# The first layer of three 512-row expert blocks as seven products of halves

## The chip, the cores and the metric

The kernel runs on one core of one Trainium2 chip. The metric is the time of one execution on the device in microseconds (us), from the first to the last instruction with what the launch puts around it. A time "of the runs" is the median of several executions; a profiled execution is a single one, with its own time.

## The reference

A Fourier mixing of eight sequences is followed by a layer of eight experts, of which each row uses one.

```python
# x: (8, 2496, 256)
X = np.fft.fft(np.fft.fft(x, axis=1), axis=2)
x = X.real.reshape(19968, 256)              # rows for the experts
logits = x @ w_gate                         # (19968, 8)
expert_idx = np.argmax(logits, axis=1)
gate_w = softmax(logits)[np.arange(N), expert_idx]
for e in range(8):                          # rows of expert e
    h = np.maximum(x_sorted[lo:hi] @ w1[e], 0.0)   # 256 -> 1024
    y_sorted[lo:hi] = h @ w2[e]                    # 1024 -> 256
out = gate_w[:, None] * y_sorted[inv_perm]
```

All of it is in float32. Only the counts of rows per expert depend on the data.

## The kernel before, in words

**Mixing.** Each of the eight batches of 2496 rows is transformed in two steps. `first(b)` folds the input on VectorE (tile `xq`, lines 307 to 324), multiplies by waves on TensorE (PSUM tile `s1`), copies to `t1` on ScalarE and writes it to DRAM (`Td`). `regroup` reads it back as `t4s`. `second(b)` works on 128 transformed rows at a time: two products `p2` (shown as `p<-table,t4s`), a copy to `zz`, two products `p3` (`p<-table,zz`), copies `zs` and `lg` on ScalarE, the rows themselves on VectorE (line 480) and their mirrored half on ScalarE (line 454). `turn_last` is a small product `pr` and its copy. After five such groups `route` picks each row's expert (`oh`), finds its rank among the rows of that expert by the products `rk`, and queues ten sends. `send` (line 532) copies an index on ScalarE (`due`), casts it on GpSimd (`pi`) and scatters 128 rows to the buffer `Xs` in DRAM, where rows of one expert lie together. `plan` (line 548) then makes, on one partition, the table of blocks of the next round.

**Experts.** The rows of a batch, as far as they fill whole blocks, are worked on in the round of that batch: batch 2 has three blocks of 512 rows of one expert, batches 3 to 7 five each (the first two batches and the tail use blocks of 256 and 128). `experts` is a generator that runs over the blocks. For each block it fetches rows (`xb`, line 606) and weights (`w1_sb`, `w2_sb`, 1 MB each) through the SyncE queue, some blocks ahead; `turn` (line 648) transposes `xb` to `xT` on VectorE (line 654) and negates the odd half on ScalarE (line 657). The first layer then makes `hT` from `xT` and the weights, the second makes `py` from `hT`, which ScalarE scales to `y` (line 962) and GpSimd scatters to the output.

**Two ways for the first layer.** The plain way (lines 899 to 914) makes, for each of eight tiles of 128 hidden units, `ph` with two instructions of 512 columns; ScalarE and VectorE take turns with the relu (lines 910 and 908). The other way is `seven` (line 685): the contraction (256), the hidden units (1024) and the rows (512) are halved, and seven products of halves take the place of eight. For that, `right` makes four sums of parts of `xT` (lines 642 to 645) and `Left` four of parts of the weights (line 637), all on VectorE. Two passes `g` of seven products each accumulate into PSUM tiles `a` to `e`; the results are put together by five additions on VectorE (lines 706, 709, 712, 720, 725) and five copies or relus on ScalarE (703, 716, 717, 722, 726). Which blocks use it says `halved(b, size)`, line 193. `quartered` (line 198) says which blocks do the second layer by seven products too: those that `halved` names in the last batch, or with a number of 3 or more in their batch.

**What sets the order.** Instructions are issued in program order on each engine. The generators of the mixing and of the experts are woven by the loop at line 1066. Each `yield w, full` of `experts` tells how much of a block was done; a yield that isn't `full` adds `ticks * w / ((SHARE if b >= LATE else EARLY) * open_)` to `due`, and each whole tick runs one step of the mixing of the next batches, and for early rounds one send. The steps of `seven` yield `0.5, True`, the plain first layer `1, False`, the second layer `2, False` per 128 rows, or `1, False` twice where `halved`. `open_` (line 1075) counts 8 for a halved block and 16 for another, so that the ticks of a round sum up to the same. When the next block is halved, its `right` comes from `turn`, and its `Left` either from the steps of the present `seven` or, after a plain block, at the end of it (line 967).

**Buffers.** [...] `pm_` has three for all of the mixing, `pse` one for each of the five names `a` to `e`; `ph` uses `a` and `c`, `py` uses `b` and `d`. `xT`, `xs` and `hT` have one buffer each, `ws` two, `xb`, `w1_sb`, `w2_sb` and `y` three, `due` eight.

Of the kernel before, what the change touches and what calls it, by code (L numbers as in the profile page):

```python
# [20 lines left out]
B, S, D = 8, 2496, 256  # L21
# [170 lines left out]

def halved(b, size):

    return size == 512 and b > 2 or size == 256 and b == B - 1


def quartered(b, size, at):

    return halved(b, size) and (b == B - 1 or at >= 3)  # L200
# [17 lines left out]
def kernel(ctx: ExitStack, tc, x, w_gate, w1, w2, out):  # L218
# [429 lines left out]
    def turn(b, size, xb):  # L648


        xT = bp.tile([128, 2, BIG], F32, tag="xT", name="xT", bufs=1)
        n = min(size, 256)
        for h in range(-(-size // 256)):
            vec.transpose(free(xT[:], 256 * h, [32, n // 32], [BIG, 2], [1, 32]),  # L654
                          free(xb, 512 * h, [64, n // 32], [1, 2], [2, 32]))
            odd = xT[:, 1, 256 * h:256 * h + n]
            act.activation(odd, odd, ACTF.Copy, scale=-1.0)  # L657
            yield xT
        if halved(b, size):
            th = size // 2  # L660
            xs = bp.tile([128, 3, th], F32, tag="xs", name="xs", bufs=1)
            r = right(xs, *(xT[:, c, k * th:(k + 1) * th] for c in range(2) for k in range(2)))
            yield r
# [136 lines left out]
    def experts(todo):  # L800
# [44 lines left out]
        for k, (b, size, last, at) in enumerate(todo):  # L845
# [20 lines left out]
            if follow and got and halved(follow[0], follow[1]):  # L866
                more = Left(got[0][0])
# [282 lines left out]
```

## Time and profile before

| | |
|---|---|
| median of three runs | 1253.59 us (1252.57 to 1254.63) |
| the profiled execution, its own time | 1256.62 us |
| its span, first to last instruction | 1254.8 us |
| TensorE clock granted over the span | 0.981 |
| busy TensorE, VectorE, ScalarE, GpSimd | 1210.5, 761.5, 431.8, 448.0 us |
| batch 2's three blocks, first to last product | 238.5 to 338.2 us |
| moved by DMA | 248.32 MB, 198 GB/s |

The profile is of one execution. In the names of engines PE is TensorE, PEld its weight loads, DVE VectorE, ACT ScalarE, POOL GpSimd and SPq the queue of transfers that SyncE issues. A line of a timeline gives the start, the duration, the engine, the line of the kernel, the operation, the tiles (written from read), their shapes and a count; in brackets stands how long the engine was idle before, and what it waited for. All matmuls have line 223, that of a helper, so they are told apart by tiles. A float32 matmul instruction appears as two passes, so that counts of TensorE are twice those of the code. A line of the chain of waits gives the start, the time until the next piece, and the engine and tile that the end of the program hung on. In the rows of digits each digit is the busy share of a fortieth of the span, in tenths.

### The profile page before, as it was taken

The page shows a single profiled execution, that of the slowest core. Times are in us where ns is not written, and L with a number is a line of the kernel's source. Part 1 is how long each engine was busy: PE and PEld are TensorE (multiplying, and loading weights), DVE is VectorE, ACT ScalarE, POOL GpSimd, SP SyncE. Part 2 cuts the span into 40 slices and gives each one's busy share as a digit, 9 for nine tenths or more (in the row PEclk, how much of TensorE's full clock was granted, in tenths as well). Part 3 has the DMA queues.
Part 4 walks back from the last instruction along what each step waited for, and adds up shares of the span by engine and source line. Part 5 has one row for each costly group of instructions (what it writes and reads, how often), then busy time and mean ns, then how long its engine had stood idle before and what let it go on. Part 6 is the DMA issues. An engine that isn't in the chain of part 4 may idle for free.

```text
span 1254.8 us, 22389 instructions
## 1 busy us (share of the span) xinstructions
PE 1210.5 (96%) x7317; PEld 1077.9 (86%) x7317; DVE 761.5 (61%) x1820; ACT 431.8 (34%) x1168; POOL 448.0 (36%) x531
## 2 busy tenths in 40 slices
PE   7569999999999999999999999999999999999997
PEld 5458888777788899889988899889999999999996
DVE  4745334343556787566865488686888884444663
ACT  2334333333244433434343433432332332222222
POOL 0426336163126421471226612471463241111112
PEclk8779999999999999999999999999999999999998
DMA  8679899873649443763347435443446238788887
GB/s 235 186 257 347 293 310 309 229 255 99 150 154 271 135 141 119 203 217 112 101 129 216 134 115 172 134 156 98 126 134 192 93 114 302 271 282 292 277 285 270
DMA packets 163062, 248.32 MB, mean 198 GB/s; under 512 B 118542, under 2 KB 130200, under 8 KB 143473
## 3 DMA queue, kind: packets, MB, share of 16 engines
q1 hardware_dynamic: 145644, 201.79, 50.8%
q0 software_dynamic: 16080, 42.85, 9.6%
q10 hardware_dynamic: 1221, 2.24, 0.6%
q8 instruction: 59, 0.97, 0.3%
q14 instruction: 58, 0.48, 0.1%
HBM read 193.45 MB, written 53.45 MB: 197 GB/s over the span
## 4 chain that ended last, share of the span: by engine, by line
PE 65%; issue 17%; DVE 8%; DMA 4%; POOL 3%; ACT 2%; SPq 0%; POOLq 0%; DVEq 0%; ACTq 0%
PE py L223 19%; PE a L223 9%; PE c L223 8%; PE ph L223 7%; PE p L223 6%; PE b L223 5%; PE d L223 4%; PE e L223 3%; PE s L223 3%; POOL out_dram L238 3%; DMA xq<-in_x_dram 2%; DVE xT L654 1%; DMA Td<-t 1%; DMA t4s<-Td 1%; DVE y L754 1%
## 5 line engine op out<-in xcount | busy, mean ns | idle before, releaser
L238 POOL DMA_INDIRECT out_dram<-y,ro x163 | 161.6, 991 | 627.6 <-ACT y L750 302.9
L223 PE MATMUL py<-w_sb,hT 128*128 128x256 f32 x1504 | 340.0, 380 | 0.4 <-DVE hT L908 0.4
L223 PEld LDWEIGHTS py<-w_sb,hT 128*128 128x128 f32 x1504 | 281.3, 190 | 37.6 <-issue 1.0
L238 POOL DMA_INDIRECT Xs<-rows,pi x160 | 161.8, 1011 | 87.5 <-POOL pi L539 42.6
L223 PE MATMUL ph<-xT,w_sb 128*128 128x128 f32 (+2 forms) x992 | 170.9, 328 | 4.7 <-DVE ro L863 4.7
L223 PEld LDWEIGHTS ph<-xT,w_sb 128*128 128x128 f32 x992 | 136.6, 192 | 28.7 <-issue 16.8
L480 DVE SCALAR_TENSOR_TENSOR rows<-p,zs 128x129 f32<-128x129 f32 x160 | 48.8, 347 | 128.2 <-ACT lg L478 122.1
L223 PE MATMUL a<-xT,w_sb 128*128 128x256 f32 (+1 forms) x512 | 117.9, 357 | 0.2 <-DVE xT L654 0.2
L908 DVE TENSOR_SCALAR hT<-ph 128x512 f32<-128x512 f32 x43 | 29.7, 691 | 134.5 <-PE ph L223 74.8
L223 PEld LDWEIGHTS a<-xT,w_sb 128*128 128x128 f32 x512 | 88.6, 190 | 10.2 <-DVE xT L654 0.6
L962 ACT ACTIVATE y<-py,xb 128x256 f32<-128x256 f32 x94 | 44.6, 474 | 151.5 <-PE py L223 151.3
L657 ACT ACTIVATE xT<-xT 128x256 f32<-128x256 f32 (+1 forms) x94 | 36.5, 389 | 173.8 <-DVE xT L654 131.9
L706 DVE TENSOR_TENSOR hT<-hT,b 128x512 f32<-128x512 f32 x57 | 39.2, 688 | 75.7 <-PE b L223 49.2
L716 ACT ACTIVATE hT<-a 128x512 f32<-128x512 f32 x57 | 34.0, 597 | 134.2 <-PE a L223 129.7
L539 POOL CAST pi<-due 128x1 int32<-128x1 f32 x140 | 43.8, 313 | 70.2 <-ACT due L538 70.2
L223 PE MATMUL a<-w_sb,hT 128*128 128x128 f32 x528 | 66.0, 276 | 0.0
L223 PEld LDWEIGHTS a<-w_sb,hT 128*128 128x128 f32 x528 | 63.1, 192 | 0.7
L223 PEld LDWEIGHTS p<-table,t4s 120*128 120x128 f32 x352 | 54.4, 205 | 10.9 <-ACT t4s L442 3.4
L223 PE MATMUL p<-table,zz 128*128 128x145 f32 (+1 forms) x320 | 57.1, 302 | 5.0 <-DVE rows L480 2.2
L223 PE MATMUL c<-xT,ws 128*128 128x256 f32 (+1 forms) x256 | 60.3, 362 | 0.8
L223 PE MATMUL p<-table,t4s 120*128 120x120 f32 (+1 forms) x352 | 57.8, 290 | 3.4 <-ACT t4s L442 2.6
L223 PE MATMUL b<-xs,ws 128*128 128x256 f32 (+1 forms) x256 | 58.7, 356 | 0.0
(163 smaller groups left out, 2063.6 us busy)
## 6 DMA issues: line engine op xcount, KB each, us to landing
w_sb<-in_moe_w_dram SPq DMA_DIRECT2D x132, 1024.0 KB
xq<-in_x_dram SPq DMA_DIRECT2D x23, 896.0 KB
xb<-Xs SPq DMA_DIRECT2D x112, 128.0 KB
Td<-t SPq DMA_DIRECT2D x18, 448.0 KB
t4s<-Td SPq DMA_DIRECT2D x7, 768.0 KB
t4s<-Td SPq DMA_DIRECT2D x7, 640.0 KB
xb<-Xs SPq DMA_DIRECT2D x52, 64.0 KB
xb<-Xs SPq DMA_DIRECT2D x88, 32.0 KB
```

Of the source, the lines that this page charges most:

```text
L223: nc.tensor.matmul(o, lhsT=lhsT, rhs=rhs, start=start, stop=stop, **kw)
L238: return unordered(pool.indirect_dma_start(out=dst, out_offset=bass.IndirectOffsetOnAxis(ap=idx, axis=0), in_=rows, in_offset=None, bounds ...
L480: vec.scalar_tensor_tensor(rows[:, k + m, 0:NY], p3[:, 0:NY], zs[:, 0:1], zs[:, 1:], op0=ALU.add, op1=op)
L539: pool.tensor_copy(idx, due[:])
L654: vec.transpose(free(xT[:], 256 * h, [32, n // 32], [BIG, 2], [1, 32]), free(xb, 512 * h, [64, n // 32], [1, 2], [2, 32]))
L657: act.activation(odd, odd, ACTF.Copy, scale=-1.0)
L706: vec.tensor_tensor(h12, h11, b[:], op=add)
L716: act.activation(h11, a[:], ACTF.Relu)
L754: vec.tensor_tensor(o, o, p[:], op=add)
L908: vec.tensor_scalar(o, ph[:], 0.0, None, op0=ALU.max)
L962: act.activation(y[:, i % 2], py[:], ACTF.Copy, scale=meta[:, i, 1:2])
```

## The change

`halved` is asked by `turn`, by `experts` and by the loop that weaves. It now says yes for every block of 512 rows, where it did so from batch 3 on. Batch 2 is the only earlier batch with such blocks, so its three blocks use `seven` for the first layer, and the second layer of these blocks yields twice per 128 rows. The numbers of the blocks are 0 to 2, so `quartered` stays false for them.

```diff
 def halved(b, size):
 
-    return size == 512 and b > 2 or size == 256 and b == B - 1
+    return size == 512 or size == 256 and b == B - 1
```

The function that then makes the first layer, as it stands in both kernels (cut):

```python
        for g in range(half // fp):
            a, b, c, d, e = (pse.tile([128, fp, th], F32, tag=k, name=k) for k in "abcde")
            h11, h12, h21, h22 = (q[:, g * fp:(g + 1) * fp] for q in quarters(hT, size))
            product(g, 0, a)
            act.copy(h11, a[:])
            yield
            product(g, 5, b)
            vec.tensor_tensor(h12, h11, b[:], op=add)
            yield
...
            product(g, 2, c, False)
            vec.tensor_tensor(h12, h12, c[:], op=add)
            act.activation(h12, h12, ACTF.Relu)
            ends(g)
            step()
            yield
```

## Prediction

> **What bounds the kernel now.** I read the page's busy times and slices first, then the chain of work that ended last over batch 2's round (238 to 338 us), then the timelines of VectorE, ScalarE and the SyncE queue around the instructions that the change moves.
>
> ```profile
> PE 1210.5 (96%) x7317; PEld 1077.9 (86%) x7317; DVE 761.5 (61%) x1820; ACT 431.8 (34%) x1168; POOL 448.0 (36%) x531
> PE   7569999999999999999999999999999999999997
> PEclk8779999999999999999999999999999999999998
> ```
>
> TensorE is busy in every slice after the third at nearly full clock; VectorE has 39% of the span free and the others more. In the stretch 238.47 to 338.23 us PE is busy 99.76 of 99.76 us at clock 1.00, DVE 39.35, ACT 31.15, POOL 36.30, the DMA engines 57%. So the round is priced in TensorE time. The chain shows a whole first layer of a 512-row block of batch 2, and one as seven products (batch 3's first block):
>
> ```profile
> 274.29 13.73 PE ph L223 x32
> 288.02 6.91 PE py L223 x32
> ...
> 338.23 0.86 PE a L223 x4
> ...
> 350.32 3.45 PE py L223 x16
> ```
>
> Each x counts the two passes that TensorE makes of one of these instructions. The old layer is 32 passes of 128x512 in 13.73 us, the new one 14 steps of four passes of 128x256, from 338.23 to 350.32, 12.09 us, each step 0.86, with no idle time between steps and none before the second layer (py). This is already with the additions on VectorE and the relus on ScalarE between products, so they keep up when no other work is mixed in.
>
> [...] If halving the moving side made the weight load the limit, seven products would win nothing. The trace says no: a pass of 256 columns is 0.86/4 = 216 ns, one of 512 is 13.73/32 = 429 ns, and a weight load is 190 ns, just under the first. [...] So I don't take 99.76 us as proof that no wait is in it, but compare starts of equal steps.
>
> **The change, part by part.**
>
> *Removed and added on TensorE.* Three blocks give up 13.73 us and take 12.09: 3 x 1.64 = 4.92 us gained. The second layer isn't touched: its other condition (a block number of at least 3, or the last batch) is false for the blocks 0 to 2 of batch 2.
>
> *Added on VectorE and ScalarE.* Per block VectorE gets ten additions instead of four relus (6 x 0.69), four subtractions on xT (4 x 0.42) and four on the weights (4 x 0.68): 8.5 us, 25.6 in the round, so 39.35 becomes about 65 of 95 us. ScalarE gets ten instructions of 0.6 instead of four, 3.6 us a block, 42 of 95 us. Neither becomes the bound; what matters is where they stand. For the first block the eight subtractions stand while the 256-row block before is in its second layer:
>
> ```profile
> 233.59 0.12 DVE L863 CAST ro<-xb 128x4 int32<-128x4 f32 x1
> 242.16 0.69 DVE L908 TENSOR_SCALAR hT<-ph 128x512 f32<-128x512 f32 x1 [8.45 <-issue]
> ...
> 326.39 0.42 DVE L642 TENSOR_TENSOR xs<-xT 128x256 f32<-128x256 f32 x1
> 329.86 0.68 DVE L637 TENSOR_TENSOR ws<-w_sb 128x512 f32<-128x512 f32 x1
> ```
>
> They take 4 x 0.42 + 4 x 0.68 = 4.4 us of that 8.45 us gap. The second half of xT is negated by 236.0, so they end near 240.0; the first product (238.5) needs none of the weight sums, the second (239.3) the two done by 238.7, the third (240.2) the one done by 239.3. I cost this at nothing; without the cover it is up to 240.0 - 238.5 = 1.5 us. For blocks 2 and 3 the weight sums are made inside the previous first layer, as in later rounds.
>
> *Moved: the other work of the round.* The outer loop gives the mixing of batches 3 and 4 in ticks. A step of a seven-product layer gives none, so all 32/0.7 = 45.7 ticks fall in the second layers, 1.9 per half row group (1.73 us) where it was 1.9 per whole one (3.45 us). Its TensorE pieces remain the same: 8.0 us in block 1, 4.8 in block 2, 3.9 in block 3. The built order shows two places where they stand closer than before.
>
> Place 1, block 3's second layer: two pairs of mixing products and a pr stand behind each other with no ph between. Now ph stands ahead of them:
>
> ```profile
> 311.15 0.44 PE p L223 x4
> 311.59 0.12 PE pr L223 x2
> 311.70 0.60 PE p L223 x4
> ```
>
> ScalarE's part, from the timeline of two stretches of the next round:
>
> ```profile
> 361.41 0.27 ACT L475 COPY zs<-p 128x130 f32<-128x130 f32 x1
> 361.73 0.40 ACT L454 COPY rows<-rows 128x254 f32<-128x254 f32 x1
> ...
> 412.27 0.42 ACT L657 ACTIVATE xT<-xT 128x256 f32<-128x256 f32 x1 [0.65 <-DVE xT L654]
> ```
>
> The p after pr gets the PSUM buffer of the p before it, so it waits for that one's copy to zz. ScalarE has ahead of this copy the negation of xT, which starts 2.2 us after the first layer's end (412.27 against 410.07), then zz of the pair before (2.55), zs (3.02), rows (3.34), lg (3.65) and it itself (3.71 to 4.0), at the steps of that timeline, of which 361.41 to 361.73 is one. TensorE wants the p at 1.73 + 0.95 + 0.44 + 0.12 = 3.24. Wait: 0.7 us, bounds 0.3 and 1.2 (0.3 if ScalarE's copies overlap more; 1.2 if xT is late by half a microsecond). Behind it on TensorE stands all the rest of the layer, so it counts in full.
>
> Place 2, block 1's second layer: the four subtractions on xT (1.67 us) now stand between the last rows and the choice of the expert (oh), for which the rank products (rk) wait. The same stretch one round later, without them in between:
>
> ```profile
> 369.66 0.24 DVE L501 TENSOR_TENSOR oh<-table,v 128x80 bf16<-128x80 f32 x1
> ```
>
> and TensorE:
>
> ```profile
> 371.68 0.20 PE L223 MATMUL rk<-oh,tri 128*128 128x88 bf16 x1
> ```
>
> The slack is 371.68 - 369.90 = 1.78 us, the insert 1.67: 0.1 us, bounds 0 and 0.5.
>
> *Queues.* The SyncE queue's order of transfers is unchanged. GpSimd's sends of batch 3's rows (20 x 1.45 us: cast 0.20, gap 0.28, 0.97) are given in some 45 us of second layers; it lags by about 4 us behind block 1, and eight index buffers and three pairs of y rows absorb this: cost nothing, up to 0.5.
>
> *Sum.* 4.92 - 0.7 - 0.1 = 4.1 us. The profiled execution took 1256.62 us (span 1254.8 and 1.8 around it), 3.03 above the median of 1253.59; 1256.62 - 4.1 = 1252.5 for it, 1249.5 for the median.
>
> **The rivals.**
>
> Rival 1: the crowded second layers cost more, as some ten mixing products that now follow another with half the TensorE work between wait 0.27 us each for ScalarE's copies, with three PSUM buffers: 2.7 us in place of 0.8. For it: ScalarE takes about 1.7 us for the copies of one pair. Against: in batch 3's first block (350 to 372 us) the same crowding shows no wait over 0.1 us. Time: 1253.59 - 4.92 + 2.7 = 1251.4.
>
> Rival 2: the gain is given back later at a wait that runs on a transfer's own time (a weight load, t4s, the rows of batch 3). For it: DMA engines 57% busy in the round. Against: after 123 us TensorE never waits over 0.8 us until the last ten, and those two waits (417.6 and 563.2) are for ScalarE's copy behind VectorE, which move along. Time: 1253.6.
>
> Rival 3, slower: the rows of batch 3's first block come too late. The transpose for that block stands on VectorE, and its negation on ScalarE, ahead of the copies that mixing products of block 3's second layer wait for, so lateness stops TensorE one for one.
>
> ```profile
> 307.41 0.33 SPq L411 DMA_DIRECT2D Td<-t  x1
> 310.19 2.63 SPq L606 DMA_DIRECT2D xb<-Xs  x4
> 313.02 2.97 SPq L610 DMA_DIRECT2D xb<-Xs  x1
> ```
>
> Now they are fetched behind Td and are there about 316.2 (the transfers fall from 163 to 55 GB/s at 316), used at 325.1. After the change, Td's rows are made 3.5 us earlier, so the rows are there near 312.7; the first layer ends at 238.5 + 3 x 12.09 + (13.81 + 8.1) + (13.81 + 4.8) = 315.3, and the transpose comes at 316.7. Slack 4.0 us. It costs from 4.0 us of lateness on, and the kernel is slower by over 2.5 us from 4.0 + 4.1 + 2.5 = 10.6 us on: 1256.5. For it: the slack falls from 8.9 to 4.0 us. Against: nothing in the order delays the fetch.
>
> That the change doesn't do what it says is excluded: the built order has 42 two-instruction products in the round in the place of 48 ph instructions of 512 columns.
>
> **How the numbers follow.** Forecast 0.72 (1248.4 to 1250.6), all faster. Rival 1 0.13 (0.07 faster, 0.06 same). Rival 2 0.10 (0.04 faster where a part is given back, 0.06 same). Rival 3 0.05 (0.04 slower, 0.01 same). A measurement tells about 0.2%, 2.5 us, from no change. Faster 0.83, same 0.13, slower 0.04. The range goes from the full gain less scatter of the median (1248.67 - 0.3) to rival 1, 1251.4; what lies above and below is under 2 in 10.
>
> **What would show it.** Three first layers of 12.1 us (14 steps of 0.86) and none of 13.7; batch 3's first product near 334.1 instead of 338.23; a TensorE wait of about 0.7 us behind pr in block 3's second layer and nearly none ahead of the second rk; later stretches as long as now. A wait at the first b of block 1, many waits of 0.3 us behind ScalarE in the second layers, or a VectorE wait for xb near 317 us would make it wrong.

## The result and the profile after

The changed kernel takes 1251.45 us (median of 21 runs, 1245.42 to 1256.19), the kernel before, run beside it, 1255.05 (21 runs, 1252.26 to 1262.78). The ratio is 0.9966, 95% interval 0.9954 to 0.9978: 4.3 us less, between 2.8 and 5.8 (the two medians lie 3.60 us apart, the two means 4.48). The forecast was 4.1 us less.

The profiled execution took 1254.30 us, its span 1252.5 at clock 0.977. The first two lines of the page after:

```profile
span 1252.5 us, 22624 instructions
PE 1209.7 (97%) x7389; PEld 1094.7 (87%) x7389; DVE 786.0 (63%) x1862; ACT 441.7 (35%) x1186; POOL 451.8 (36%) x531
```

TensorE has 72 passes more (7317 to 7389: 3 blocks x (14 x 4 - 32)) and VectorE 24.5 us more work. TensorE's busy time is hardly less, and the span is only 2.3 us shorter. Neither is a measure of the change: the start, in which TensorE waits for transfers, was 2.3 us longer in the execution after (the tile t4s had landed at 67.2 us before, at 69.6 after), and nothing of the change stands there. What the change did is read from the chain of waits, from batch 2's first product to batch 3's. The round begins, before, with

```profile
238.63 5.15 PE ph L223 x12
```

and ends with the product a at 338.23 that the prediction shows. Of after:

```profile
240.71 0.86 PE a L223 x4
...
252.80 3.45 PE py L223 x16
...
274.80 0.86 PE a L223 x4
...
286.89 10.36 PE py L223 x48
...
321.38 0.77 PE p L223 x4
...
336.05 0.86 PE a L223 x4
```

Where a ph of 13.73 us stood, there are 12.09 us from the first product a to the second layer's py (240.71 to 252.80; 274.80 to 286.89). The round takes 336.05 - 240.71 = 95.34 us, where it took 338.23 - 238.63 = 99.60: 4.26 less. The chain gives these starts 0.16 us later than TensorE's timeline does (240.71 and 240.55 for the same product), so a difference is taken within one of the two. The stretch table of after, one line per stretch (the round, the rest; TensorE, its weight loads, VectorE, ScalarE, GpSimd, then granted clock, DMA share and GB/s):

```profile
240.55:335.89 95.34, 94.90 (x502) 84.31 (x501) 60.97 (x156) 41.23 (x119) 38.38 (x52) 1.00 0.60 186
335.89:1252.50 916.61, 906.08 (x5748) 830.88 (x5746) 609.75 (x1304) 320.36 (x795) 323.20 (x356) 1.00 0.55 181
```

The same rest in the stretch table of before:

```profile
338.07:1254.80 916.73, 905.68 (x5748) 831.03 (x5746) 609.72 (x1304) 320.57 (x795) 322.08 (x356) 1.00 0.55 181
```

It is 916.61 us after and 916.73 before, so the gain isn't given back; and from t4s to the round it is 170.99 us where it was 171.25. In the round VectorE went from 39.35 to 60.97 us, ScalarE from 31.15 to 41.23. TensorE has 0.44 us without work where it had none; its timeline of after shows the one place (in brackets the wait and its cause):

```profile
320.67 0.28 PE L223 MATMUL pr<-t4s,table 120*120 120x5 f32 x2
321.38 0.77 PE L223 MATMUL p<-table,zz 128*128 128x145 f32 x4 [0.44 <-ACT zz L449]
```

That is place 1 of the prediction. The bracket counts only the time without any product. From start to start this p comes 0.71 us after pr, where it came 0.14 us after it before (311.42 and 311.56 in TensorE's timeline), because there it starts while pr, 0.28 us long, is still running. So the place costs 0.57 us. ScalarE's timeline of after shows the copies ahead of it:

```profile
320.43 0.27 ACT L475 COPY zs<-p 128x130 f32<-128x130 f32 x1
320.59 0.41 ACT L454 COPY rows<-rows 128x254 f32<-128x254 f32 x1
...
320.96 0.37 ACT L449 COPY zz<-p 128x240 f32<-128x240 f32 x1
```

At place 2 there is no wait. At the start of block 1 VectorE's timeline of after shows where the eight subtractions went, of which these are the second and the fourth weight sum and the first addition behind them:

```profile
239.97 0.69 DVE L637 TENSOR_TENSOR ws<-ws,w_sb 128x512 f32<-128x512 f32 x1
...
241.18 0.68 DVE L637 TENSOR_TENSOR ws<-w_sb,ws 128x512 f32<-128x512 f32 x1
...
242.55 0.69 DVE L706 TENSOR_TENSOR hT<-hT,b 128x512 f32<-128x512 f32 x1 [0.61 <-PE b L223]
```

The second one is done at 240.66, and the second product, which reads it, starts at 241.41: 0.75 us left. The last is done at 241.86, and VectorE is idle again before the addition.

### The profile page after: what moved, and what is told of

It is laid out like the page before. It is cut to its first block, busy times and chain, and to the rows that moved or that the text cites. A ratio compares the mean times of both kernels' runs of the same rounds, so it can differ in the third digit from the quotient of the medians.

```text
span 1252.5 us, 22624 instructions
## 1 busy us (share of the span) xinstructions
PE 1209.7 (97%) x7389; PEld 1094.7 (87%) x7389; DVE 786.0 (63%) x1862; ACT 441.7 (35%) x1186; POOL 451.8 (36%) x531
## 4 chain that ended last, share of the span: by engine, by line
PE 83%; DVE 8%; DMA 3%; ACT 2%; issue 2%; SPq 0%; POOL 0%; POOLq 0%; DVEq 0%; ACTq 0%
PE py L223 24%; PE a L223 12%; PE c L223 11%; PE ph L223 9%; PE b L223 6%; PE p L223 6%; PE d L223 6%; PE e L223 5%; PE s L223 4%; DMA xq<-in_x_dram 2%; DVE xT L654 1%; DVE y L754 1%; DVE hT L709 1%; DVE hT L712 1%; DVE hT L706 1%
## 5 line engine op out<-in xcount | busy, mean ns | idle before, releaser
L223 PE MATMUL ph<-xT,w_sb 128*128 128x128 f32 (+1 forms) x896 | 127.7, 300 | 4.7 <-DVE ro L863 4.7
L223 PE MATMUL a<-xT,w_sb 128*128 128x256 f32 (+1 forms) x560 | 130.3, 359 | 0.3 <-DVE xT L654 0.3
L223 PEld LDWEIGHTS ph<-xT,w_sb 128*128 128x128 f32 x896 | 118.8, 193 | 11.1 <-DVE ro L863 5.1
L223 PEld LDWEIGHTS a<-xT,w_sb 128*128 128x128 f32 x560 | 97.6, 190 | 11.7 <-DVE xT L654 0.9
L908 DVE TENSOR_SCALAR hT<-ph 128x512 f32<-128x512 f32 x31 | 21.4, 690 | 104.1 <-PE ph L223 52.3
L223 PE MATMUL c<-xT,ws 128*128 128x256 f32 (+1 forms) x280 | 66.4, 364 | 0.9 <-DVE hT L712 0.2
L223 PE MATMUL b<-xs,ws 128*128 128x256 f32 (+1 forms) x280 | 65.0, 359 | 0.0
L223 PE MATMUL d<-xT,w_sb 128*128 128x256 f32 (+1 forms) x280 | 64.9, 358 | 0.0
L223 PE MATMUL e<-xs,w_sb 128*128 128x256 f32 (+1 forms) x280 | 64.9, 358 | 0.0
L223 PE MATMUL c<-xs,ws 128*128 128x256 f32 (+1 forms) x280 | 64.9, 358 | 0.0
```

The source lines that it names most:

```text
L223: nc.tensor.matmul(o, lhsT=lhsT, rhs=rhs, start=start, stop=stop, **kw)
L908: vec.tensor_scalar(o, ph[:], 0.0, None, op0=ALU.max)
```

## The experiments

My theory: the gain is TensorE's time in the first layer, three times 1.64 us, less the crowding that the new order of the mixing brings (place 1); the work added on VectorE costs nothing as long as the gaps it lies in are there. Its rivals: the order or something else of the weaving makes the gain or eats more of it; the cover on VectorE is thicker or thinner than read; the rows of batch 3 are nearly late. Ratios are to the kernel before, run beside each group.

**1. The new weaving alone.** Plain first layers, but ticks given as in the changed kernel; nothing of the computation changes.

```diff
+def crowded(b, size):
+    return halved(b, size) or size == 512
...
-                yield 1, False
+                yield (7 / 8, True) if crowded(b, size) else (1, False)
...
-                        if f == FC // 2 - 1 and halved(b, size):
+                        if f == FC // 2 - 1 and crowded(b, size):
```

The yield of 1 in place of 2 per half row group and the list of blocks ask `crowded` too; `halved` is as before.

> The kernel before with the plain first layer in batch 2's blocks, but with the changed kernel's weaving: the first layer gives no ticks, the second gives them all, twice per 128 rows. My theory (the gain is in the TensorE time of the seven products, the weaving only costs): first layers stay at 13.7 us each, the round from batch 2's first product to batch 3's first takes 99.6 plus 0.4 to 0.7 = about 100.1 us, the time 1.000 to 1.001 of before. Rival (the gain comes from the closer weaving): the round is at 95 to 97 us and the time at 0.997.

Measured: 1257.38 us beside 1256.55, ratio 1.0002 (0.9988 to 1.0016). Its chain of waits, where the helper of the matmuls is line 228:

```profile
240.66 13.73 PE ph L228 x32
...
326.01 0.27 ACT zz L454
...
326.32 0.77 PE p L228 x4
...
340.99 0.86 PE a L228 x4
```

The round takes 340.99 - 240.66 = 100.33 us, 0.73 more than before, and the chain goes through ScalarE's zz in the same place as in the changed kernel (a wait of 0.49 us). So the order by itself costs 0.7 us, and seven products in it give 100.33 - 95.34 = 4.99 us, against 4.92 by the steps' durations. The two terms of the sum are measured apart, with one reserve: the way to this zz isn't the same. In the changed kernel the chain comes to it from VectorE's last weight sum, the transpose and the negation of xT. Here there is no weight sum, xT is early, and ScalarE waits for TensorE's p ahead of the copies (0.32 and 0.20 us). That both cost nearly the same may be chance.

**2. Mixing spread over the seven products too.** In the early rounds a step of `seven` gives ticks, so the mixing doesn't crowd in the second layers.

```diff
-                    yield 0.5, True
+                    yield 0.5, b > 2
...
-        open_ = sum(k * (8 if seven_ else 16) for _, k, seven_ in blocks)
+        open_ = sum(k * ((8 if b > 3 else 15) if seven_ else 16) for _, k, seven_ in blocks)
```

> The changed kernel with the mixing of the other batches spread over the first layers of batch 2's blocks too, in proportion to the work. My theory: the 0.44 us wait behind pr in block 3's second layer goes, as the pairs stand apart; the seven products are then mixed with other work of VectorE and ScalarE. If these keep up: round 94.9 us, 0.4 below the changed kernel's 95.3, time 0.996 of before. Rival (the additions need VectorE and ScalarE undisturbed, which is why these layers give no ticks): products wait for additions that stand behind mixing work, the round is 1 to 3 us longer than 95.3, time 0.997 to 0.999.

Measured: 1251.83 us, ratio 0.9966 (0.9953 to 0.9979); the round 332.86 - 236.17 = 96.69 us, 1.35 longer than in the changed kernel. The wait behind pr is 0.1 us, but block 3's first layer has a new one. TensorE's and then VectorE's timeline:

```profile
317.92 1.13 PE L223 MATMUL c<-xT,ws 128*128 128x256 f32 x4 [1.58 <-DVE hT L712]
```

```profile
312.87 0.23 DVE L494 TENSOR_REDUCE mx<-lg 128x10 f32<-128x80 f32 x1
...
315.52 0.17 DVE L312 COPY xq<-xq 104x8 f32<-104x8 f32 x1
...
317.18 0.69 DVE L712 TENSOR_TENSOR hT<-hT,c 128x512 f32<-128x512 f32 x1
```

With the mixing came its choice of the expert and its folding (line 494 to 312), 2.7 us on VectorE, ahead of the additions that empty the PSUM tile c. By the round, the crowding of the second layers is the cheaper place for it; the times of the runs don't tell the two kernels apart (0.9966 both).

**3. The cover of block 1 taken away.** The first weight sum of batch 2's first block is made five times instead of once (that `Left` is called with 4, and the loop behind the second layer makes sums until none is left); the values are unchanged.

```diff
-        def __init__(self, w1_sb):
+        def __init__(self, w1_sb, more=0):
...
+            self.due.extendleft([self.due[0]] * more)
```

> The changed kernel with the first of the weight sums for batch 2's first block made five times instead of once (4 more vector operations of 0.6 to 0.7 us with the same result). My theory: the sums end at 241.9 in the changed kernel's profile, the one that the second product (241.4) waits for at 240.7, so the cover has 0.75 us left; 2.6 us more makes the second product wait 1.8 us, the round goes from 95.3 to 97.1 us, and the time rises by 1.8 us. Rival (VectorE's idle 8.45 us cover it, 4 us are left): round unchanged at 95.3.

Measured: 1253.36 us, ratio 0.9973 (0.9963 to 0.9983). TensorE's timeline:

```profile
237.99 1.03 PE L223 MATMUL a<-xT,w_sb 128*128 128x256 f32 x4
241.15 1.10 PE L223 MATMUL b<-xs,ws 128*128 128x256 f32 x4 [2.13 <-DVE ws L638]
```

VectorE runs the five sums one after another from 236.69 to 240.31, 0.72 us each. In the changed kernel the first two of the four sums start 0.72 us apart too, where the second reads what the first wrote, and the others 0.60 and 0.61; here each writes the tile of the one before. The second product waits 2.13 us: the four added sums, 4 x 0.72 = 2.88, less the 0.75 that the changed kernel has left. The round takes 335.69 - 237.99 = 97.70 us by TensorE's timeline, 2.36 more than the changed kernel's, where 97.1 was expected; the sums were longer than expected. The times of the runs (0.9973 against 0.9966) don't tell the two apart. So the cover is as thin as that timeline says: the subtractions are free there, and anything over 0.75 us more isn't.

**4. Batch 1's 256-row blocks by seven products as well.** This asks whether the price per column holds for passes of 128 columns.

```diff
-    return size == 512 or size == 256 and b == B - 1
+    return size == 512 or size == 256 and b > 0
```

(`quartered` is kept as it was.)

> The changed kernel with seven products also in the first layer of the four 256-row blocks of batch 1's round. My theory (a product is priced by its columns): passes of 128 columns take 112 ns as in the later second layers (16 in 1.79 us), a first layer 56 x 0.112 = 6.3 instead of 6.9 us, four blocks gain 2.6 us, less 0.5 to 1.5 for crowding in a stretch where copies already wait: time 0.995 of before. Rival (the 190 ns weight load sets the pace of short passes): a layer takes 56 x 0.19 = 10.6 us, 15 us more in all, time 1.008 of before.

Measured: 1255.58 us, ratio 0.9996 (0.9983 to 1.0009): slower than the changed kernel (0.9966 beside its own group). The steps themselves are as priced, 7 x 0.89 = 6.25 us where a plain layer takes 6.91, so weight loads don't limit passes of 112 ns here; they overlap: a load beside passes of 128x128 takes 192 ns on average in the trace of before, and eight of them one after another would fill 1.54 us where a step of eight passes takes 0.89. From 187.75 to 191.70 us TensorE and its weight loads are both busy without a gap (3.95 us each). But two of four such layers wait at product d for a weight sum (line 637), 2.45 us at 187.75 and 2.66 us at 226.93. TensorE's timeline of the second and of the steps after it:

```profile
226.93 1.59 PE L223 MATMUL d<-xT,w_sb 128*128 128x128 f32 x8 [2.66 <-DVE w_sb L637]
228.31 1.92 PE L223 MATMUL c<-xs,ws 128*128 128x128 f32 x8
230.02 1.48 PE L223 MATMUL a<-xT,w_sb 128*128 128x128 f32 x8
231.34 1.06 PE L223 MATMUL e<-xs,w_sb 128*128 128x128 f32 x8
```

Only two of the four weight sums are made in the layer before; the others stood on VectorE behind work of the mixing: planning (lines 514 to 564) at the first wait, the choice of the expert and the folding (lines 494 to 501, 310 to 312) at the second. After the second wait three steps take 4.41 us (226.93 to 231.34) instead of 2.68: the granted clock was 0.50 from 227.5 to 230.9. From batch 1's first such layer to batch 2's first product it is 78.75 us, and 74.01 in the changed kernel: +4.74. From start to start the two d come 2.62 and 2.83 us late, so 2.62 + 2.83 + 1.73 - 4 x 0.66 = 4.5 are named.

**5. The rows of batch 3's first block fetched three times.** The same rows into the same buffer, so each set waits for the one before; nothing is computed differently.

```diff
-        for q in range(4):
+        for q in list(range(4)) * (3 if b == 3 and i == 0 else 1):
```

> The four quarter transfers of the rows of batch 3's first block are issued three times, so that the rows are there later by some 5 to 6 us (each set of four takes 2.7 us from the row fetch's start to the next one). My theory: the rows came about 4 to 4.5 us before VectorE's transpose wanted them, so 5 to 6 us of lateness uses that up and the rest, 1 to 2 us, stops TensorE one for one in block 3's second layer (a wait at p or pr behind ScalarE's part of xT): round 96 to 98 us, ratio to before 0.997 to 0.999. Rival A (the slack is longer than read, or the transfers overlap): VectorE shows no wait for xb before its transpose, the round stays at 95.3 us, ratio 0.9966. Rival B (the lateness also pushes the weights and t4s behind it on the SyncE queue): waits in batch 3's first block too, round plus 5 us or more, ratio 1.000 or above.

Measured: ratio 1.0023 (1.0010 to 1.0035). This group ran on a chip on which the kernel before takes 1267.51 us, and whose traces have waits in other rounds that the first chip's don't have; so I use the round. VectorE's and TensorE's timelines:

```profile
327.51 0.71 DVE L654 STREAM_TRANSPOSE xT<-xb 128x512 f32<-128x512 f32 x1 [4.85 <-DMA xb<-Xs]
```

```profile
329.03 0.56 PE L223 MATMUL pr<-t4s,table 120*120 120x5 f32 x2 [4.59 <-ACT zz L449]
...
330.97 3.55 PE L223 MATMUL py<-w_sb,hT 128*128 128x256 f32 x8
```

The transpose was 4.85 us late, later than I had meant (I had taken the issue time of a set for its duration), and TensorE waited 4.59 us there and 0.24 at the next p, behind ScalarE's zz, by the path that rival 3 named. The round took 346.69 - 242.94 = 103.75 us, 8.41 more than the changed kernel's, in three parts. pr starts 7.87 us after the first layer's end instead of 3.12, and the p behind it 0.1 later still: 4.85 us, the lateness one for one. The p and the py behind it take 2.18 us longer, since the clock was 0.50 from 327.5 to 334.3 (the py of eight passes 3.55 instead of 1.89). And block 2's first layer is 1.37 us longer, with waits of 0.24 and 0.31 us that stand ahead of the late rows; experiment 6 on the same chip, which leaves the rows alone, has one of 1.15 us in that layer. The mechanism of my theory held, its size didn't. The ratio and the round are those of rival B, but its sign, waits in batch 3's first block, isn't there.

**6. The 256-row blocks with all four sums made early.** Experiment 4 with two more `step()` in each of these layers.

```diff
+            if size == 256 and not both:
+                step()
...
+                if size == 256:
+                    step()
```

> The 256-row blocks of batch 1 by seven products as in the experiment before, with two more weight sums made inside each of their first layers, so that all four for the next block are done in it. If the 2.45 and 2.66 us waits at product d came from sums that stood behind planning work on VectorE, they go, and each such layer gains the 0.66 us that its TensorE time promised (6.91 to 6.25): the stretch ahead of batch 2's first product shortens from 57.7 us (from 182.98) to about 55.5, and the kernel is 2 to 2.6 us faster than the changed one, ratio to before 0.9945 to 0.995. Rival: VectorE is then too full inside these short layers (eight additions, relus, four weight sums of 0.68 in 6.25 us), and the products wait for PSUM tiles that VectorE hasn't emptied: ratio 0.997 or above.

Measured on the slower chip: ratio 1.0014 (0.9995 to 1.0033), with waits of 2.91 and 1.15 us at c in these layers but also of some 2 us in rounds that this edit doesn't touch. Inconclusive; repeated below as 9.

**7. Only batch 2's first block by seven products.** `halved` gets the block's number and, of batch 2, says yes for block 0 alone; the loop that weaves counts one halved block and two plain ones.

```diff
-    return size == 512 or size == 256 and b == B - 1
+    return size == 512 and (b > 2 or at == 0) or size == 256 and b == B - 1
```

> Only batch 2's first block makes its first layer by seven products; blocks 2 and 3 are plain. If the gain is the TensorE time of each block (1.64 us) and the costs sit in block 3's second layer alone, the round falls from 99.6 us to about 98.0, at most 98.3 with a small wait at the rank products, and the ratio to before is 0.9985 to 0.999. Rival: if the gain came from the order (weaving) or from the passage from block to block and not from each layer, the round is at 99 or more or at 97 or less.

Measured: ratio 0.9960 (0.9939 to 0.9981), 8 runs on the slower chip. The expected 0.9985 to 0.999 lies outside this interval: the whole run gained more than one block explains, and no run shows why. The round is as expected: 338.99 - 240.74 = 98.25 us, in the 98.0 to 98.3. So one block gives 1.35 us of its 1.64 against the 99.60 of the kernel before (a trace of the first chip). At the start of block 3's first layer a p, which now stands close behind pr, waits 0.19 us for the copy of t4s and starts 0.43 us late; in the changed kernel a py stands between the two. So the gain is made in the layer and not in the passage from block to block.

**8, 9 and 10. The changed kernel, the repeated experiment 6, and the rows fetched twice, on one chip** (the kernel before: 1255.45 us).

> The changed kernel itself, as a measure for the two kernels beside it on the same chip. Both theories expect 0.9966 of before, interval of some 0.0012 to each side, and a round of 95 to 96 us; if the chip is one on which the kernel before takes some 1267 us, waits for VectorE's sums of up to 2 us stand in the first layers too, and the round may be 96 to 99 us.

> The kernel with batch 1's 256-row blocks by seven products and all their weight sums made in the first layer before, now beside the changed kernel on one chip. Theory: the four layers' 2.6 us are won, 0.998 of the changed kernel, 0.9945 of before, with no wait of over 0.5 us at product d in batch 1's round. Rival: on a full VectorE new waits (at product c, for the addition after it) take the gain, and the time is that of the changed kernel or above it.

> The four quarter transfers of the rows of batch 3's first block issued twice. With three sets VectorE's transpose came 4.85 us late, so each further set delays the rows by about 4.7 us (14.6 us from the first of the three sets to the end of the last), and the slack in the changed kernel is about 2 x 4.7 - 4.85 = 4.6 us. Theory: with two sets the rows come 0 to 0.5 us late, so the wait behind pr grows from 0.44 us by at most 0.5 us, and the ratio is that of the changed kernel, 0.9966, within 0.0012. Rival: transfers share the DMA engines and the slack is used up earlier; the wait is 1 us or more and the ratio 0.9975 or above.

Measured for 8: ratio 0.9953 (0.9934 to 0.9971), round 338.34 - 243.01 = 95.33 us, with the same one wait (0.44 us): the changed kernel's round repeats to 0.01 us.

Measured for 9: ratio 0.9969 (0.9951 to 0.9987), not told apart from 8. The 2.45 and 2.66 us waits are gone, and two others are there:

```profile
193.26 1.16 PE L223 MATMUL c<-xT,ws 128*128 128x128 f32 x8 [0.88 <-DVE hT L714]
...
231.08 1.16 PE L223 MATMUL c<-xT,ws 128*128 128x128 f32 x8 [1.14 <-DVE hT L714]
```

The stretch from batch 1's first such layer to batch 2's first product is 239.15 - 165.16 = 73.99 us, 74.01 without the edit. Of the 2.64 us that TensorE's time promised, 2.36 go to these two places (from start to start the two c come 1.05 and 1.31 us late), and the rest to single steps of 0.1 us more. The rival was right: in both layers VectorE had about 3 us of the mixing's work ahead of the first addition, and weight sums made inside the layer stand ahead of the later ones. Done this way, the 256-row blocks won nothing that these runs show.

Measured for 10: ratio 0.9979 (0.9960 to 0.9997), round 338.06 - 241.01 = 97.05 us, 1.72 more than 8. The waits there are longer by 1.47 us, now at pr itself, with 0.43 at the p behind it; they were expected to grow by at most 0.5, so the numbers are the rival's. Its chain of waits shows both sets of rows:

```profile
309.32 7.08 DMA xb<-Xs
...
318.23 2.72 DMA xb<-Xs
...
321.07 0.72 DVE xT L654
```

One set lands at 316.40, 7.08 us after its issue, and VectorE would be free for the transpose at 319.34. So the slack is 2.9 us with one set (2.7 by the same reading of experiment 5), and neither the 4.0 of the prediction nor the 4.6 of this expectation. The expectation took 4.7 us for each set; the second set lands 4.55 us after the first, but the third of experiment 5 only 2.8 after its second. Beyond the slack lateness stops TensorE one for one: the transpose 1.73 us late, the round 1.72 longer.

## Why the prediction was right

- *Removed and added on TensorE, 4.92 us.* Right: 12.09 us per layer, and 4.99 for the three by experiment 1 against the changed kernel. Experiment 7 shows 1.35 us for one block.
- *TensorE has no wait before.* Right, but the 99.76 us take the start from the timeline and the end from the chain; within one of them the round is 99.60.
- *Neither VectorE nor ScalarE becomes the bound.* Right for 512-row blocks (60.97 and 41.23 of 95.34 us; 65 and 42 were forecast). Experiment 2 shows that this is a matter of place and not of the sum: with about 64% of the round VectorE stops TensorE where 2.7 us of mixing work stand ahead of an addition. Experiments 4 and 9 show the same in batch 1's round.
- *The first block's subtractions cost nothing.* Right; the last ended 1.31 us after the first product's start (241.86 against 240.55; 1.5 was forecast), and the one that the second product reads was done 0.75 us ahead of need. Experiment 3 shows the price without cover.
- *Place 1, 0.7 us.* Right in place and path, 0.57 in size, of which 0.44 show as a wait. The negation of xT starts 2.21 us after the first layer's end (319.76 against 317.55), as forecast; then ScalarE's copies follow each other in less time than in the rows of the next round from which I added them: zs follows zz by 0.35 us and not 0.47, rows follows zs by 0.16 and not 0.32. So zz of the second p starts 3.41 us after the first layer's end (320.96 against 317.55) and not 3.71. The negation isn't needed for such a wait: in experiment 1 xT is early, and the place waits 0.49 us all the same.
- *Place 2, 0.1 us.* No wait: oh was done at 270.63 and rk ran at 270.79.
- *Sum, 4.1 us.* 4.26 by the round, 4.3 by the ratio: 4.92 - 0.57 leaves 0.09 us in smaller differences. In absolute time the forecast fits less well: 1251.45 us lie above the 1249.5 of the forecast and just past the end of its range, 1251.4. It was counted from the 1253.59 us of three runs, and the kernel before took 1255.05 beside the changed one, so 1.46 of these 1.95 us were there without the change. The ratio is the fair comparison.
- *Rival 1* (crowding costs 2.7 us) falls: 0.73. *Rival 2* (given back later) falls: 916.61 against 916.73 us. *Rival 3* didn't happen, and experiments 5 and 10 show that its path is real and that its slack is 2.9 us and not 4.0: I had put the landing of the rows at the end of a busy stretch of transfers, 6.0 us after their issue, shifted by the earlier Td; measured, it took 7.08 us. The chance of 0.05 rested on a margin that was 1.1 us too wide.
- *Batch 3's first product near 334.1* was a bad sign to name: it was at 336.05, because the start of that execution was 2.3 us longer. The length of the round is the sign to look at.

## What to carry to other kernels

Where TensorE is busy without gaps, price the change by the durations of its own steps in the same trace, and compare lengths between equal steps, not spans: here the round repeated to 0.01 us, while the medians of whole runs needed 20 runs to show 4 us. Count a wait from start to start: the idle time in brackets leaves out some 0.1 to 0.2 us by which a product otherwise starts under the one before (0.14 us behind pr; 0.17 behind a step of 1.03 us that the next follows after 0.86). Then ask of each added instruction on another engine what stands right behind it and how long until TensorE needs that; VectorE at 64% was free in one place and cost 1 to 2 us in the next. An earlier first layer also brings forward what must be loaded by its end, so measure that slack by making the load later and not from a traffic curve.

## What the runs showed of the hardware that I had not expected

In these runs a TensorE wait sometimes cost more than its length. After the waits of 2.66 us (experiment 4), 2.80 and 4.59 us (experiment 5), and 2.91 and 3.31 us (experiment 6), the granted clock fell to 0.50 for 3.4 us, with the one of 4.59 for 6.8, the first 1.5 of them still within the wait; in part it fell only about 1 us after work had resumed (it was still 1.00 in the 0.95 us behind the wait of 2.80). The lower clock cost 1.73 us in experiment 4 and 2.18 in experiment 5. A line of experiment 4's stretch table after its wait of 2.66 us, the clock being the third number from the right:

```profile
228.00:229.00 1.00, 1.00 (x7) 1.00 (x7) 0.58 (x2) 0.00 (x0) 0.00 (x0) 0.50 0.80 157
```

The length of a wait alone doesn't decide here. The clock stayed at 1.00 after 1.47 us (experiment 10), 1.58 (experiment 2), 1.96 (experiment 6), 2.13 (experiment 3) and 2.45 us (experiment 4), and it fell after 1.98 us in experiment 6 and 1.13 us in experiment 7. Products took longer behind waits of 1.70 us in experiment 6 (a py of 16 passes 4.40 us instead of 3.62) and of 1.16 us in experiment 5 (a ph of 16 passes 3.38 us instead of 1.95). TensorE's timeline and then the stretch table of experiment 7:

```profile
133.78 1.26 PE L223 MATMUL p<-table,zz 128*128 128x145 f32 x4 [1.13 <-ACT lg L478]
```

```profile
135.00:136.00 1.00, 1.00 (x7) 1.00 (x6) 0.00 (x0) 0.40 (x2) 0.00 (x0) 0.50 1.05 279
```

What decides whether the clock falls behind a wait, no run here shows.
